# A written-out order for the second attention front and the inverse steps ahead of it

## The chip, the core and the metric

The kernel runs on one core of a Trainium2 chip. Its time is the device time of one execution in microseconds (us). The kernel before was run 12 times: the median is 447.94 us, the lowest 445.24, the highest 451.13. One execution was also recorded by the profiler.

The engines that matter here are TensorE (PE in the views; PEld is its weight load), VectorE (DVE), ScalarE (ACT), GpSimd (POOL) and SyncE (SP, which issues the DMAs). Each works through its own instructions in the order in which the program lists them, and waits at an instruction until what it needs is there.

## What is computed

Four layers work on `x`, 2048 rows of 512 columns, in turn: attention, convolution, attention, convolution, each on the layer-normed `x` and added to it.

```python
x = x + _A_ref(_layernorm(x), A_wqkv, A_wo)          # attention: 32 heads of 16, window of 8 keys, dilation 2
x = x + _B_ref(_layernorm(x), ...)                   # long convolution per column, by FFT
x = x + _A_ref(_layernorm(x), A_wqkv, A_wo)
x = x + _B_ref(_layernorm(x), ...)
```

The kernel does the convolution as matrix products with Fourier factors: two forward steps, a pointwise product, two inverse steps. The change is about the seam between the first convolution's inverse steps and the second attention's first part.

## The kernel before

**The convolution's end.** `FftB` keeps the 512 columns as two groups `g` of 256. The first inverse step (`i1`, L781, written "y" in the order strings) makes one of 8 tiles per group: 16 matmuls (L792, L793) into one PSUM tile of 128 x 1024 f32, then one eviction (`evac`, L708, traced as L709) into `z`. I number these tiles y0 to y15; y0 to y7 belong to group 0 and y8 to y15 to group 1. (Group 0's `z` lies in the buffer `xnT`, so the profile calls it `xnT`.)

The second inverse step (`i2`, L797, "z") makes one of 4 blocks of 512 rows for one group; I write z10 for group 1, block 0. It needs all eight y tiles of its group. It comes in two forms. With "D", 8 matmuls (L808, L809) are followed by an addition on VectorE that adds the PSUM tile to `x_sb` (L812). With "A", 4 matmuls by the identity (L807) put `x_sb` into the sum first, and ScalarE copies the 12-matmul result back (L814).

**PSUM.** All y and z tiles come from two pools, "right" and "left", of two such tiles each, used two by two in turn (`ptile`, L704). A tile can be started when the tile that had its buffer is evicted. `swap_psum` (L848) gives the right pool up, and the front's tiles (two for transposes, two for projections) take its place.

**The attention's front.** For each block `b` of 512 rows: the statistics of each half of the columns (`half_stats`, L99: 4 instructions, L101), the mean and variance (`aggr`, L1283), the reciprocal root by Ln and Exp on ScalarE (`rstd_act`, L104), the normalisation on VectorE (`norm`, L1291, traced as L136 and 4 of L148), 16 transposes on TensorE in two tiles (`front_t`, L209; L215) with one eviction each (L218), four key projections of 4 matmuls each (`front_k`, L224; L229) with an eviction on ScalarE each (L232), and a shifted copy of the keys for the window (`front_ext`, L234; L242). The queries of a block are four projections of the same size (`qproj1`, L168; L172) with an eviction on ScalarE each (L174). The logits are then made in `core` (L295): `mult` (L277; L283, 2.3 us on VectorE) and `lsum` (L286; L290, 32 small matmuls) for each block and quarter of the columns.

I use the same short names for both kernels: h10 are the statistics of group 1 in block 0, a0, p0 and n0 the aggregation, root and normalisation of block 0, T0 its transposes, E00 and E01 their two evictions, P00 to P03 its key projections, Q00 to Q03 its query projections, x0 and e0 its shifted copies (e for the last block, by quarter), mult 00 and L00 the first product and the first logit sum.

**What sets the order.** VectorE, ScalarE, TensorE and SyncE are listed in `MAN`: they take their instructions exactly as the Python code calls them. The convolution's calls come from a string of tokens (`ORDER0`) that `run` (L819) walks through. Its last line ends in

```python
yA m m yA m yA yD yD yD yD yD zD yA yA zD yA yA zD zD zD
```

where A and D say whose eviction it is. Behind it the front is written as Python: `i2(1, 1)`, statistics, normalisation and so on block after block, with one of each block's transpose evictions on ScalarE and one on VectorE, and 4 spare matmuls (`warm`, L193; L195) after the first transposes. Block 3's keys and block 0's queries are called from `core`'s events around the first `mult`s.

Of the kernel before, what the change touches and what calls it, by code (L numbers as in the profile page):

```python
# [14 lines left out]
F32 = mybir.dt.float32  # L15
# [5 lines left out]
P = 128  # L21
S = 2048
D = 512
# [4 lines left out]
NDT = 4  # L28
# [9 lines left out]
NG = 2  # L38
DQG = 64
EC = 16  # L40
NEC = 128 // EC
# [3 lines left out]
KA KD KA KD KA KA KD KA KD KA KD kA KD KA KA kD kA kD kA UA KD UA UA UD UA kD UA  # L45
UA UD KA UA kD u kD m u u u kA m UA m UD UA u kA m kD u UA u m UA m
UD m UA kA u kD kD u kA u m m kA m u u yD yA m u u m u m yA u yA
yA m m yA m yA yD yD yD yD yD zD yA yA zD yA yA zD zD zD
"""
ORDER1 = """  # L50
UD UA UA UD UA UA UD UA UD UA UD u UD u m UA u u m UA m u u UA m UD m
u u m m m u u m u m m u u m u m m u yA yA yA m u yA yA yA yA
m yD yA yD yD yA zD yD yA zD yA yA zD zD zD zD zA zB
"""

def build_a_consts(tc, nc, cpool, tpool):
# [42 lines left out]
def half_stats(nc, lnst, x_sb, t, g):  # L99
    for a in range(4 * t, 4 * t + 4):  # L100
        nc.vector.bn_stats(lnst["bn"][:, a, g, :], x_sb[:, a, g * (D // 2):(g + 1) * (D // 2)])  # L101
# [49 lines left out]
class LayerA:  # L151
# [31 lines left out]
    def front_open(self):  # L183
        tc = self.tc
        self.fctx = ExitStack()
        l = self.layer
        self.fp = self.fctx.enter_context(tc.tile_pool(name=f"a{l}_front", bufs=2, side="right"))
        self.ps_tr = self.fctx.enter_context(tc.tile_pool(name=f"a{l}_ps_tr", bufs=2, space=PSUM, side="right"))
        self.ps_pj = self.fctx.enter_context(tc.tile_pool(name=f"a{l}_ps_pj", bufs=2, space=PSUM, side="right"))
        self.pj_tag = "pp"  # L190
        self.nc.gpsimd.memset(self.kT[:, :, 0:14, 0:1], 0.0)

    def warm(self, ps, n, rhs):  # L193
        for _ in range(n):
# [11 lines left out]
        for a in range(4):  # L206
            ln_apply(self.nc, self.xn[:, a, :], x_rows[:, a, :], rn[0], rn[1], a, ln_eng[a])

    def front_t(self, b, ev_eng, defer=False):  # L209
        nc, xn, evs = self.nc, self.xns.pop(b), []  # L210
        for dp in range(2):
            pt = self.ps_tr.tile([P, 2, 4, P], BF16, name="pt")
            for di in range(2):
                for a in range(4):
                    nc.tensor.transpose(pt[:, di, a, :], xn[:, a, (2 * dp + di) * P:(2 * dp + di + 1) * P], self.c["ident"][:])  # L215
            dst = self.xnT[:, 2 * dp:2 * dp + 2, b * 512:(b + 1) * 512]
            f = nc.scalar.copy if ev_eng[dp] == "act" else nc.vector.tensor_copy
            evs.append(lambda f=f, dst=dst, pt=pt: f(dst, pt[:].rearrange("p t a q -> p t (a q)")))  # L218
        if not defer:
            for f in evs:  # L220
                f()
        return evs

    def front_k(self, b, ev_eng, fts=range(NDT)):  # L224
# [445 lines left out]
class FftB:  # L670


    def __init__(self, tc, nc, C, ident, w2_dram, g2_dram, kf_dram, x_sb, tag):
        self.tc, self.nc, self.C, self.ident, self.kf_dram, self.x_sb = tc, nc, C, ident, kf_dram, x_sb
        self.w2_dram, self.g2_dram = w2_dram, g2_dram
        self.tag = tag
        self.c_grp, self.c_mid, self.c_ps = ExitStack(), ExitStack(), ExitStack()
        self.grp = self.c_grp.enter_context(tc.tile_pool(name=f"b{tag}_grp", bufs=5, reuse_waits="tile"))
        self.ps = [c.enter_context(tc.tile_pool(name=f"b{tag}_ps_{side}", bufs=2, space=PSUM, side=side))
                   for c, side in ((self.c_ps, "right"), (self.c_grp, "left"))]  # L680
        self.npt = 0
        self.kf, self.nat, self.ub = {}, {}, {}
        self.nkf = 0
        g2p = self.c_grp.enter_context(tc.tile_pool(name=f"b{tag}_g2", bufs=1, reuse_waits="tile"))
        self.g2 = g2p.tile([P, 2, 16, P], BF16, name="g2_sb")
        self.S = [dict() for _ in range(NG)]
# [107 lines left out]
        self.evac(z[:, :, t * DQT * 4:(t + 1) * DQT * 4].rearrange("p m (j d) -> p m j d", d=4),  # L794
                  p3[:].rearrange("p j (m d) -> p m j d", d=4), eng)

    def i2(self, g, t, eng="dve", defer=False):  # L797

        nc, x_sb = self.nc, self.x_sb
        z = self.S[g]["z"]  # L800
        dsl = slice(g * DQG * 4, (g + 1) * DQG * 4)
        p4 = self.ptile([P, 4, DQG * 4])
        n_add = {"dve": 4, "both": 2, "act": 0}[eng]
        for j in range(4):
            a = t * 4 + j
            if j >= n_add:
                nc.tensor.matmul(p4[:, j, :], lhsT=self.ident[:], rhs=x_sb[:, a, dsl], start=True, stop=False)  # L807
            nc.tensor.matmul(p4[:, j, :], lhsT=self.g2[:, 0, a, :], rhs=z[:, a, :], start=(j < n_add), stop=False)  # L808
            nc.tensor.matmul(p4[:, j, :], lhsT=self.g2[:, 1, a, :], rhs=z[:, NA + a, :], start=False, stop=True)  # L809
        if n_add:  # L810
            xr = x_sb[:, t * 4:t * 4 + n_add, dsl]
            nc.vector.tensor_tensor(xr, p4[:, 0:n_add], xr, ALU.add)  # L812
        if n_add < 4:
            ev = lambda: nc.scalar.copy(x_sb[:, t * 4 + n_add:t * 4 + 4, dsl], p4[:, n_add:4])  # L814
            if defer:
                return ev
            ev()

    def run(self, order, u, done=lambda g, t: None, k=None, late=()):  # L819
        late, cnt = list(late), {}  # L820
        src = dict(K=("ka", k), U=("ua", u))
        self.nk, self.nm = (0, 0) if k is not None else (NG * NEC, 0)
        self.pump()
        for tok in order.split():
            op, eng = tok[0], dict(A="act", D="dve", B="both").get(tok[1:])
            n = cnt[op] = cnt.get(op, -1) + 1
            g, t = divmod(n, 4 if op == "z" else 8)
            if op in src:
                key, x = src[op]
                self.f1(g, x, key, t, eng)  # L830
                if op == "K":
                    if n > 0 and late:
                        late.pop(0)()
                    if n == NG * NQT - 1:
                        self.open_ring()
            elif op == "k":
                self.k_f2(g, t, eng)
            elif op == "u":
                self.u_f2(g, t)
            elif op == "m":  # L840
                self.u_mult(g, t)
            elif op == "y":
                self.i1(g, t, eng)
            else:
                self.i2(g, t, eng)
                done(g, t)

    def swap_psum(self):  # L848
        self.c_ps.close()
# [14 lines left out]
def k_gen(tc, nc, ident, ins, kd, la, x_v, lnst, b_consts, C):  # L864
# [4 lines left out]
    with ExitStack() as ctx:  # L869
# [3 lines left out]
        c0 = pw.tile([P, 2, 4 * P], BF16, name="c_t")  # L873
        xb, ln = {}, {}
        la.front_open()

        def x_load(b):
            xb[b] = la.fp.tile([P, 4, D], BF16, name="x_blk")
# [13 lines left out]
            la.front_apply(b, xb[b], ln[b], [eng] * 4, xb[b])  # L892

        def front(b):
            la.front_t(b, ["act"] * 2)
            if b == 0:
                x_load(2)
            la.front_k(b, ["act"] * 4)
            if b < 3:
                la.front_ext(b, "dma")  # L900
# [267 lines left out]
def kernel(  # L1168
# [92 lines left out]
    fb.ahead = 4  # L1261
    fb.open_mid()
    with tc.manual_schedule(engines=MAN):
        def half(g, t):
            if g == 0 and t < 2:
                half_stats(nc, lnst, x_sb, t, 0)

        fb.run(ORDER0, u, half, kp, late)
    fb.c_mid.close()
    la.close()  # L1270
    la = LayerA(tc, nc, consts, lnst, A_wqkv, A_wo, 1, xnT, 1)
    la.front_w()
    with tc.manual_schedule(engines=MAN):
        fb.swap_psum()
        la.front_open()
        ln, agg = {}, {}

        def stats(b):
            half_stats(nc, lnst, x_sb, b, 1)
            if b > 1:  # L1280
                half_stats(nc, lnst, x_sb, b, 0)

        def aggr(b):  # L1283
            agg[b] = lnp.tile([P, 4, 2], F32, name="ln_ag")
# [6 lines left out]
        def norm(b):  # L1291
            la.front_apply(b, x_sb[:, b * 4:(b + 1) * 4, :], ln_end(nc, lnp, ln[b]), ["dve"] * 4)

        def keys(b, *fts):
            la.front_k(b, ["act"] * 4, fts)

        fb.i2(1, 1, "act")
        stats(0)
        aggr(0)
        power(0)  # L1300
        fb.i2(1, 2, "act")
        ev3 = fb.i2(1, 3, "act", True)
        norm(0)
        pt = la.front_t(0, ("act", "dve"), True)
        stats(1)
        pt[0]()
        pt[1]()
        ev3()
        la.warm(la.ps_pj.tile([P, 512], F32, name="pp", tag=la.pj_tag), 4, la.wqk[:, 0, 0:512])
        for b in range(3):  # L1310
            if b == 0:
                aggr(1)
                power(1)
                norm(1)
            keys(b, 0, 1, 2)
            pt = la.front_t(b + 1, ("act", "dve"), True)
            pt[0]()
            if b < 2:
                stats(b + 2)
            pt[1]()  # L1320
            keys(b, 3)
            if b < 2:
                aggr(b + 2)
                power(b + 2)
                norm(b + 2)
            if b > 0:
                la.front_ext(b - 1, "dve")
        la.front_ext(2, "dve")
        la.front_close()
        fb.c_ps.close()  # L1330
        fb.c_grp.close()
        krctx.close()

        def last(*fts):
            for ft in fts:
                keys(3, ft)
                la.qproj1(0, ft, la.qT[0], la.ps_pj, la.pj_tag)

        ext = lambda ft: lambda: la.front_ext(3, "dve", ft)
        ev = {("m", 0, ft): [ext(ft)] for ft in range(NDT)}  # L1340
        ev[("m", 0, 0)].insert(0, lambda: last(0, 1))
        ev[("q", 0, 0)] = [lambda: last(2)]
        ev[("q", 0, 1)] = [lambda: last(3)]
        ev[("p", 8)] = [lambda: la.load_w2(w2_dram)]
        la.core(x_sb, u, lnp, ev)
    la.close_logits()

# [49 lines left out]
```

## Time and profile before

| | us |
|---|---|
| median of 12 runs | 447.94 |
| profiled execution, its own time | 447.13 |
| its span, first to last instruction | 445.3 |
| TensorE busy in the span | 349.2 |
| VectorE busy | 407.4 |
| ScalarE busy | 320.5 |
| GpSimd busy | 45.1 |
| granted TensorE clock, mean | 0.987 |

The seam lies at about 256 to 303 us of the span. The y tiles of group 0 end near 260 us, those of group 1 near 270 us; the first `mult` of the second attention starts at 297.83 us. The median time of one instruction, from the groups of that stretch:

| operation | engine | ns |
|---|---|---|
| y eviction, 128 x 1024 f32 from PSUM | VectorE | 1215 |
| the same | ScalarE | 1015 |
| z addition (D form) | VectorE | 1211 |
| z copy (A form) | ScalarE | 1008 |
| transpose eviction | VectorE / ScalarE | 680 / 1014 |
| key or query eviction, 128 x 512 f32 | ScalarE | 583 |
| one half-statistic (4 for an h) | VectorE | 413 |
| one normalisation (4 for an n) | VectorE | 410 |

An instruction's recorded time is longer than its distance from the next, since the engines overlap the end of one with the start of the next: four y evictions in a row on ScalarE took 3.80 us, so the next follows after some 0.93. How to read the views: a row of the timeline is the start, the time taken, the engine and line, what is written from what, a count, and in brackets the idle time before it with what ended it.

### The profile page before, as it was taken

How to read it: one execution, taken by the hardware profiler on the slowest of the kernel's cores; microseconds unless marked ns; L12 is line 12 of the kernel's file. 1: busy time of each engine (PE TensorE's matmuls, PEld its weight loads, DVE VectorE, ACT ScalarE, POOL GpSimd, SP SyncE). 2: the span in 40 equal slices, each digit the busy share in tenths (PEclk: the TensorE clock that was granted, in tenths of full speed). 3: DMA queues.
4: the chain of work that ended last, by engine and by line, in shares of the span. 5: the costliest groups of instructions: out<-in, count | busy, mean ns of one | idle time of the engine just before them, and what ended most of it. 6: DMA issues, size and time to landing. Idle time of an engine off the chain costs nothing.

```text
span 445.3 us, 12704 instructions
## 1 busy us (share of the span) xinstructions
PE 349.2 (78%) x5455; PEld 265.3 (60%) x5494; DVE 407.4 (91%) x563; ACT 320.5 (72%) x538; POOL 45.1 (10%) x46
## 2 busy tenths in 40 slices
PE   1000045879999998999897898999999899998795
PEld 1000024566676577787787796545657687867694
DVE  6799999999999999998789999879999999889974
ACT  5979989686555559888999963764655459679862
POOL 2000101100089400000400000000000020000000
PEclk9999997999999999999999999999999899999999
DMA  7930641121411575480266730850033056224405
GB/s 207 373 114 14 69 70 27 46 55 21 103 17 41 150 252 163 129 353 16 112 231 226 254 121 24 244 159 3 2 83 85 0 202 236 87 97 133 155 25 166
DMA packets 65354, 54.17 MB, mean 122 GB/s; under 512 B 36781, under 2 KB 53778, under 8 KB 64018
## 3 DMA queue, kind: packets, MB, share of 16 engines
q1 hardware_dynamic: 65154, 53.22, 39.0%
q8 instruction: 43, 0.70, 0.7%
q10 hardware_dynamic: 144, 0.13, 0.1%
q14 instruction: 13, 0.11, 0.1%
HBM read 30.28 MB, written 13.24 MB: 98 GB/s over the span
## 4 chain that ended last, share of the span: by engine, by line
PE 32%; DVE 19%; ACT 11%; DMA 5%; issue 3%; SPq 2%; DVEq 0%; ACTq 0%
PE po L395 9%; DVE prod L283 5%; PE pq L407 4%; ACT a1s L709 4%; PE pq L336 3%; PE pq L172 3%; PE L L290 2%; DVE pav L387 2%; DVE ln_bn L101 2%; DVE t L767 2%; DMA kf_ring<-kf_dram 2%; PE pb L792 2%; PE pb L793 2%; ACT ub L779 2%; PE pp L229 2%
## 5 line engine op out<-in xcount | busy, mean ns | idle before, releaser
L387 DVE TENSOR_TENSOR pav<-attn,v_ext 128x4096 bf16<-128x4096 bf16 x32 | 72.8, 2284 | 0.5 <-DMA v_ext<-v_ext 0.2
L283 DVE TENSOR_TENSOR prod<-qT,kT_ext 128x4096 bf16<-128x4096 bf16 x29 | 66.5, 2309 | 1.1 <-ACT qT L174 0.6
L395 PEld LDWEIGHTS <-pav 128*128 128x128 bf16 x1024 | 60.4, 99 | 10.9 <-DVE pav L387 6.5
L395 PE MATMUL po<-ident,pav 128*128 128x128 bf16 x1024 | 64.0, 222 | 3.6 <-DVE pav L387 3.6
L215 PE MATMUL pt<-ident,x_blk 128*128 128x128 bf16 x64 | 5.6, 241 | 45.2 <-ACT x_blk L146 45.2
L229 PE MATMUL pp<-xnT,kT_ext 128*128 128x512 bf16 x124 | 30.5, 384 | 5.9 <-ACT xnT L218 3.8
L779 ACT CAST ub<-pb 128x1024 bf16<-128x1024 f32 x32 | 33.0, 1089 | 2.2 <-DVE t L767 2.1
L129 POOL TENSOR_TENSOR ln_rstd<-ln_rstd,ln_mh 128x4 f32<-128x4 f32 x6 | 10.0, 1658 | 233.1 <-DVE ln_rstd L128 211.1
L792 PE MATMUL pb<-Wp,t 128*128 128x128 bf16 x256 | 30.2, 219 | 2.7 <-ACT ub L779 2.2
L215 PEld LDWEIGHTS <-x_blk 128*128 128x128 bf16 x64 | 4.4, 108 | 46.3 <-ACT x_blk L146 46.0
L290 PEld LDWEIGHTS <-prod 128*128 128x128 bf16 x928 | 27.1, 96 | 8.1 <-DVE prod L283 2.5
L338 ACT CAST v_ext<-pq 128x512 bf16<-128x512 f32 x32 | 18.7, 586 | 18.0 <-PE pq L336 17.7
L727 PE MATMUL pb<-a1s,w_sb 128*128 128x64 bf16 x768 | 27.1, 193 | 5.7 <-ACT ub L779 3.5
L1092 PE MATMUL pk<-B_t,A_t 128*64 128x84 bf16 (+1 forms) x512 | 25.5, 211 | 6.6 <-issue 4.4
L336 PE MATMUL pq<-wv,xnT 128*128 128x512 bf16 x119 | 30.3, 379 | 0.4
L398 ACT CAST oT<-po 128x512 bf16<-128x512 f32 x32 | 18.6, 580 | 16.4 <-PE po L395 16.2
L172 PE MATMUL pq<-xnT,kT_ext 128*128 128x512 bf16 x121 | 30.0, 379 | 0.4 <-issue 0.2
L709 ACT CAST a1s<-pb 128x1024 bf16<-128x1024 f32 x30 | 29.3, 1079 | 1.3 <-PE pb L720 1.3
L793 PE MATMUL pb<-WpJ,t 128*128 128x128 bf16 x256 | 30.2, 219 | 0.0
L407 PE MATMUL pq<-wop,oT 128*128 128x512 bf16 x110 | 29.3, 379 | 0.9
L727 PEld LDWEIGHTS <-w_sb 128*128 128x128 bf16 x768 | 24.7, 98 | 8.1 <-issue 7.0
L1092 PEld LDWEIGHTS <-A_t 128*64 128x64 bf16 (+1 forms) x512 | 23.3, 111 | 9.7 <-issue 6.2
(222 smaller groups left out, 878.0 us busy)
## 6 DMA issues: line engine op xcount, KB each, us to landing
w_sb<-w_dram SPq DMA_DIRECT2D x8, 1024.0 KB
w_dram<-w_zero SPq DMA_DIRECT2D x1, 4096.0 KB
kf_ring<-kf_dram SPq DMA_DIRECT2D x13, 256.0 KB
kf_ring<-kf_dram SPq DMA_DIRECT2D x26, 128.0 KB
v_ext<-v_ext SPq DMA_DIRECT2D x4, 784.0 KB
x_blk<-in_A_x_dram SPq DMA_DIRECT2D x4, 512.0 KB
kT_ext<-in_A_wqkv_dram SPq DMA_DIRECT2D x4, 512.0 KB
x_sb<-in_A_x_dram SPq DMA_DIRECT2D x4, 512.0 KB
```

The lines of the kernel that those rows point to most:

```text
L172: nc.tensor.matmul(pq[:], lhsT=self.wqk[:, dt, ft * P:(ft + 1) * P], rhs=self.xnT[:, dt, q * 512:(q + 1) * 512], start=(dt == 0), stop=(dt ...
L229: nc.tensor.matmul(pp[:], lhsT=self.wqk[:, dt, D + ft * P: D + (ft + 1) * P], rhs=self.xnT[:, dt, b * 512:(b + 1) * 512], start=(dt == 0), ...
L283: nc.vector.tensor_tensor(pr, self.qT[q][:, ft].unsqueeze(1).to_broadcast([P, W, 4, P]), kap, ALU.mult)
L336: nc.tensor.matmul(pp[:], lhsT=xnT[:, dt, a * P:(a + 1) * P], rhs=wv[:, dt, :], start=(dt == 0), stop=(dt == NDT - 1))
L387: nc.vector.tensor_tensor(pv[:], attn[:, n % 4].unsqueeze(2).to_broadcast([P, W, DH, H]), vap, ALU.mult)
L395: nc.tensor.matmul(po[:, ft, :], lhsT=pvf[:, w, ft * P:(ft + 1) * P], rhs=ident[:], start=(w == 0 and ft == 0), stop=(w == W - 1), skip_gr ...
L407: nc.tensor.matmul(pw[:], lhsT=oT[:, ftp, :], rhs=wo[:, ftp, :], start=False, stop=(ftp == NDT - 1))
L709: (self.nc.scalar.copy if eng == "act" else self.nc.vector.tensor_copy)(dst, src)
L727: nc.tensor.matmul(p2[:, j, :], lhsT=self.w2[:, ec * EC + j, :], rhs=a1s[:, ec * EC + j, :], start=True, stop=True)
L779: nc.scalar.copy(ub[:], p2)
L792: nc.tensor.matmul(p3[:, j, :], lhsT=t1[:, dql, :], rhs=wp_r, start=True, stop=False)
L1092: nc.tensor.matmul(o, lhsT=lhs, rhs=Bt[:, ri, c * CH + ql].rearrange("p b g -> p (b g)"), start=(not half and j % 4 == 0 and ri == 0), sto ...
```

## The change

The end of `ORDER0` is cut off after y7, and everything up to the first `mult` is one string, `ORDERF`, that the same `run` walks through; `more` maps the front's tokens to its calls. In the tokens a digit pair after z is group and block, after h too; after E it is block and half, after P block and quarter.

```diff
-yA m m yA m yA yD yD yD yD yD zD yA yA zD yA yA zD zD zD
+yA m m yA m yA yD
+"""
+ORDERF = """
+yA yA yA yA yA yA z00D yA h00 yA z01D h01 z10A z11A h10 a0 p0 h11
+n0 z12A z02A a1 z03A h12 S T0 h02 p1 E00A n1 E01A a2 z13A P00 h13 Q00
+h03 T1 E10A p2 E11D P01 a3 P02 P03 P10 p3 P11 n2 n3 P12 T2 E20D E21A
+P13 T3 E30A P20 P21 x1 P22 P23 E31D
...
-        fb.run(ORDER0, u, half, kp, late)
+        fb.run(ORDER0, u, k=kp, late=late)
...
-        fb.i2(1, 1, "act")
-        stats(0)
-        aggr(0)
-        power(0)
-        fb.i2(1, 2, "act")
-        ev3 = fb.i2(1, 3, "act", True)
-        norm(0)
-        pt = la.front_t(0, ("act", "dve"), True)
...
-        la.warm(la.ps_pj.tile([P, 512], F32, name="pp", tag=la.pj_tag), 4, la.wqk[:, 0, 0:512])
...
+        front = dict(S=front_pools, h=lambda g, t: half_stats(nc, lnst, x_sb, t, g), a=aggr, p=power, n=norm, T=transposes,
+                     E=lambda b, d, eng: pts[b][d](eng), P=lambda b, ft: la.front_k(b, ["act"] * 4, (ft,)),
+                     Q=lambda q, ft: la.qproj1(q, ft, la.qT[q], la.ps_pj, la.pj_tag), x=lambda b: la.front_ext(b, "dve"),
+                     e=lambda ft: la.front_ext(3, "dve", ft))
+        fb.run(ORDERF, None, more=front)
...
-        ev = {("m", 0, ft): [ext(ft)] for ft in range(NDT)}
-        ev[("m", 0, 0)].insert(0, lambda: last(0, 1))
-        ev[("q", 0, 0)] = [lambda: last(2)]
-        ev[("q", 0, 1)] = [lambda: last(3)]
-        ev[("p", 8)] = [lambda: la.load_w2(w2_dram)]
+        ev = {("p", 8): [lambda: la.load_w2(w2_dram)]}
+        ev["m", 0, 0] = [last(("P", 3, 0), ("P", 3, 1), ("x", 0), ("x", 2), ("P", 3, 2), ("Q", 0, 1), ("e", 0), ("Q", 0, 2))]
+        ev["m", 0, 1] = [last(("e", 1), ("e", 2))]
+        ev["m", 0, 2] = [last(("e", 3))]
+        ev["q", 0, 0] = [last(("P", 3, 3), ("Q", 0, 3))]
```

So the four y tiles y8 to y11 and the three blocks z02, z03 and z10 go from VectorE to ScalarE; z10 and z11 come ahead of z02 and z03; block 0's second transpose eviction goes from VectorE to ScalarE, and block 2's two evictions change places (E20 on VectorE, E21 on ScalarE); block 0's first query projection is made in the front; and the 4 spare matmuls are gone. `front_open` is split so that the front's PSUM pools open at S, after z03. The order of the DMAs on SyncE's queue and of the work on GpSimd is the same in both kernels. `ORDER1`, the last convolution's string, is rewritten with explicit block numbers, in the same order as before.

## The prediction

> **What bounds the kernel now.** I read the busy table by stages first. Its columns are the length of the stretch, then busy time and count of each engine, then the granted clock.
>
> ```profile
> core 0: us, PE busy (x) PEld busy (x) DVE busy (x) ACT busy (x) POOL busy (x), PEclk, DMA share, GB/s
> 266.00:272.00 6.00, 5.44 (x66) 4.89 (x64) 5.93 (x12) 2.95 (x4) 0.00 (x0) 1.00 0.00 0
> 277.00:298.00 21.00, 18.67 (x127) 10.01 (x130) 17.62 (x59) 14.07 (x26) 0.00 (x0) 1.00 0.76 227
> 298.00:334.00 36.00, 35.58 (x489) 21.23 (x496) 33.85 (x26) 19.96 (x36) 0.00 (x0) 1.00 0.10 27
> ```
>
> At 266 to 272 VectorE is full and ScalarE half idle. At 277 to 298 none is full: the blocks hand over from one to another. Behind 298 TensorE is full. So the seam's worth is the time at which TensorE has its work behind it. The timelines tell who is late. VectorE:
>
> ```profile
> 260.90 4.61 DVE L709 CAST z<-pb 128x1024 bf16<-128x1024 f32 x4
> 270.56 3.47 DVE L812 TENSOR_TENSOR x_sb<-pb,x_sb 128x1024 bf16<-128x1024 f32 x3
> 274.06 1.41 DVE L101 BATCH_NORM_STATS2 ln_bn<-x_sb 128x6 f32<-128x256 bf16 x4
> 297.83 2.29 DVE L283 TENSOR_TENSOR prod<-qT,kT_ext 128x4096 bf16<-128x4096 bf16 x1 [0.62 <-ACT qT L174]
> ```
>
> It evicts y8 to y11, then, after z00 and z01, adds z02, z03 and z10 in one run; h10, the start of the front's chain, waits for all that until 274.06. ScalarE meanwhile:
>
> ```profile
> 257.50 3.80 ACT L709 CAST xnT<-pb 128x1024 bf16<-128x1024 f32 x4
> 265.10 1.93 ACT L709 CAST z<-pb 128x1024 bf16<-128x1024 f32 x2 [3.80 <-PE pb L793]
> 273.32 1.01 ACT L814 CAST x_sb<-pb 128x1024 bf16<-128x1024 f32 x1 [3.62 <-PE pb L809]
> ```
>
> Two holes of 3.80 and 3.62 us. The first row also gives its pitch: 0.93 us for each eviction. TensorE:
>
> ```profile
> 271.81 0.27 PE L807 MATMUL pb<-x_sb,ident 128*128 128x256 bf16 x1 [0.56 <-DVE x_sb L812]
> 276.97 1.87 PE L215 MATMUL pt<-ident,xn 128*128 128x128 bf16 x16 [1.06 <-DVE xn L148]
> 278.67 1.03 PE L195 MATMUL pp<-kT_ext,ident 128*128 128x512 bf16 x3
> 285.57 2.32 PE L229 MATMUL pp<-xnT,kT_ext 128*128 128x512 bf16 x10 [0.92 <-DVE xnT L218]
> 291.20 2.32 PE L229 MATMUL pp<-xnT,kT_ext 128*128 128x512 bf16 x10 [1.01 <-DVE xnT L218]
> 299.54 1.03 PE L172 MATMUL pq<-xnT,kT_ext 128*128 128x512 bf16 x4
> 302.93 0.22 PE L290 MATMUL L<-ind,prod 128*128 128x8 bf16 x3
> ```
>
> It waits for a PSUM buffer, for n0, and in two blocks for a transpose eviction that VectorE makes behind 8 statistics. From y15's last matmul to L01 (268.47 to 302.93) it takes 34.46 us. Its work there, by pitches of the same timeline (z of 8 matmuls 0.88, of 12 1.31, T 0.95, a projection 0.864, L00 0.80): 3 x 0.88 + 3 x 1.31 + warm 0.86 + 4 x 0.95 + 20 x 0.864 + 0.80 = 29.3. So **5.1 us are idle**.
>
> **The change, part by part.** I place the new order by those pitches, an instruction starting when its engine and its inputs are ready (a TensorE tile's result is there some 0.16 behind its pitch).
>
> *y8 to y15 on ScalarE.* It is free of y6 at 261.2 and takes y8 to y13 at 0.93 to 266.8. TensorE makes a y in 0.917 and is held to that by PSUM anyway: y8 starts at 259.5, y13 at 264.1, z00 at 265.0, y14 at 265.9, y15 at 266.8, z01 at 267.7 to 268.6. y14 and y15 are evicted at 267.0 and 267.9 to 268.95 (in the trace 269.7). Here a rule speaks against the change: the Trainium skill ("TensorEngine Tiling (Array Packing)", PSUM Bottleneck) wants both engines for evicting PSUM. Two evictors at pitches of 1.13 (the row of 4.61 for four) and 0.93 would take a tile each 0.51, 8 tiles in 4.1 us; one takes 7.4. By the rule the change loses 3.3 us. But TensorE delivers only one tile in 0.917, so one evictor at 0.93 keeps up; by the rows it costs about 0.1 and I take that.
>
> *z10 first.* TensorE z10 waits for y15 (0.4 us idle), 269.0 to 270.3; ScalarE copies it 270.5 to 271.5. VectorE, done with h01 at 271.3, starts **h10 at 271.5 instead of 274.06**. Price: z02, z03 and z10 get 4 identity matmuls each, 12 x 0.109 = 1.3 us of TensorE.
>
> *What eats most of that.* ScalarE goes z11 (271.75), p0 (273.3), z12, z02, z03 (to 276.7). VectorE: a0 to 273.2, h11, then n0 274.75 to 276.05. TensorE: z11, z12, z02, z03 to 275.5, T0 from 275.6. So T0 gains 1 us, not 2.6. The pools' swap adds a wait at T0 for z12 and z02 (evicted by 275.6), which z03 covers; without that cover T0 would be 0.1 later.
>
> *Both first evictions on ScalarE.* Queued behind z03 and p1: E00 277.0, E01 277.9 to 278.9; z13 fills TensorE meanwhile. P00 starts 278.1 and gets its second half at 279.0 (0.5 idle). In the trace P00 starts at 279.54, dense after the spare matmuls. So P00 is some 1 us ahead.
>
> *Dense from there.* Q00 to 280.3; n1 (VectorE: a1, h12, h02, n1) ends 280.7, so T1 idles 0.35; P01 to P03 to 284.0; P10's second half needs E11, which VectorE makes after h13 and h03, at 284.25, just when asked for; P11, P12 to 286.6; n2 ends 286.15, so T2 is not held; P13; n3 287.65; T3 needs E20 off VectorE (288.3), starts 288.4; P20 to P23 to 292.8; P30 to 293.65. ScalarE's evictions fit between (2 projection buffers; none late by over 0.1). P30's copy ends 294.4, e0 follows, **mult 00 at 294.8 instead of 297.83**.
>
> *The spare matmuls.* Gone: -0.86. The nearest rule is the Trainium skill's clock gate ("TensorE: Matmul & The Clock Gate", The HAM clock gate): TensorE falls to half rate after an idle window of some 3.4 us and stays there about as long. By it a cold start at T0 would stretch 3.4 us of matmuls by some 1.7 us (an estimate from that page). The rows: clock 1.00 throughout, longest idle 1.06; the new order's longest is about 0.5. I take nothing; the far end is +1.7.
>
> *Behind mult 00.* P31, P32, Q01, Q02, P33, Q03 follow on TensorE to 298.85, L00 to 299.65. mult 00 ends 297.0, e1, e2, mult 01 297.7, e3, mult 02 300.3, mult 03 302.5 (trace 305.69). From then on both kernels do the same, with TensorE full.
>
> *Moved past.* SyncE's and GpSimd's orders are unchanged. The value weights' load waits for z13 (275.6, now 277.9); its first reader is at 308.0, new 305, and all DMAs of that burst took 20 us, this one being first: covered. ORDER1 is the same order: nothing.
>
> The sum, on TensorE: work -0.86 + 1.3; start 268.6 (z01 now behind y15) for 268.47; idle 0.4 + 0.1 + 0.2 + 0.5 + 0.35 = about 1.5 for 5.1. That is +0.44 + 0.13 - 3.6 = **-3.0**; mult 00 says the same. The rest of the kernel follows its own triggers, so it shifts whole. Profiled execution: 447.13 - 3.0 = 444.1. Its time is 0.8 under the median of 447.94, so against that I put **444.9**.
>
> **Rivals.**
>
> *Handovers eat it.* The new chain is tight at n2 (0.45 spare), n3/E20 (0.1), P10 and P12. If each of the four block starts loses 0.5 us, as instructions with two waits might, 2.0 of 3.0 go: 446.9. For it: nothing full in 277 to 298 today. Against: durations there repeat within 0.02 us, and today's idle of 0.92 and 1.01 has a named cause, 8 statistics before the eviction, which the new order takes apart.
>
> *ScalarE becomes the pace.* It alone releases y8 to z13 and E00/E01: 16 evictions in one queue ahead of P00. Where ScalarE follows a projection it sits idle 0.28 before each today; if these ran at 1.01 + 0.28 = 1.29 instead of 0.93, E01 and so P00 come 16 x 0.36 = 5.8 later, for a net of +2.8: **450.7, slower**. It decides from a pitch of 0.93 + 3.0/16 = 1.12. Against: the run of four at 3.80, and TensorE tiles already waiting when ScalarE gets to them.
>
> *It is given back later.* TensorE's 35.58 of 36 moves along, but a transfer that doesn't would hold it: the copy of the values ends at 340.9 and VectorE waits for it 0.17. It is started by the values' last eviction, so it moves too. If it didn't: 447.9.
>
> **How the numbers follow.** Dense front (444.9): 0.62, own range 443.4 to 446.4. Handovers (446.9): 0.20. ScalarE's pace (450.7): 0.11. Given back (447.9): 0.07. What can be told from no change here is 0.5%, 2.24 us: faster is below 445.7, slower above 450.2. Faster: 0.53 of the first case and 0.05 of the second, 0.58. Slower: 0.09 of the third, and 0.01 each of the second, with a clock loss of 1.7, and of the fourth: 0.11. The rest, 0.31, is no change. The range, 443.2 to 448.4, leaves out the ScalarE case and the tails.
>
> **What would show it.** Right: eight L709 rows on ScalarE at 0.93 without a hole; h10 at about 271.5; T0 near 275.6; TensorE busy over 95% from 279 to 299; first L283 near 294.8; later L283 and L395 shifted by the same 3 us. Wrong: gaps before T2 or T3 named L148 or L218; ScalarE rows at 1.1 or more; a granted clock under 1.00; a first L283 at 294.8 with an end that hasn't moved.

## The result, and the profile after

The new kernel's median is 444.77 us (12 runs, 440.87 to 448.21). The old kernel, timed again beside it, has a median of 448.33 us over 49 runs. The ratio of their times is 0.9903, with a 95% interval of 0.9876 to 0.9929: **3.2 to 5.6 us shorter**. The ratio leaves out one run of each kernel (448.21 and 452.38 us) that lies more than 1.5% above that kernel's fastest. 444.9 was forecast, from a gain of 3.0.

The profiled execution of the new kernel hides this. It took 446.95 us, with a span of 445.2 against the old 445.3. A late transfer (the kernel's last swapped filter block, `kf_nat`) held VectorE for 1.45 us just ahead of y7's eviction, and TensorE for 1.36 us in y8, so the seam began late. To compare I measure the **seam**: from the start of VectorE's eviction of y7, the last instruction that both kernels share, to the start of mult 00. In the old profile it is 297.83 - 259.76 = 38.07 us:

```profile
259.76 1.23 DVE L709 CAST xnT<-pb 128x1024 bf16<-128x1024 f32 x1 [0.27 <-PE pb L793]
```

VectorE's timeline of the new kernel:

```profile
262.34 1.22 DVE L715 CAST xnT<-pb 128x1024 bf16<-128x1024 f32 x1
268.87 1.23 DVE L818 TENSOR_TENSOR x_sb<-pb,x_sb 128x1024 bf16<-128x1024 f32 x1 [5.31 <-PE pb L815]
272.79 2.80 DVE L107 BATCH_NORM_STATS2 ln_bn<-x_sb 128x6 f32<-128x256 bf16 x8
281.67 1.38 DVE L154 TENSOR_SCALAR xn<-x_sb,ln_rstd,ln_nb 128x512 bf16<-128x512 bf16 x4
285.88 0.68 DVE L226 COPY xnT<-pt 128x1024 bf16<-128x1024 bf16 x1
297.21 2.29 DVE L289 TENSOR_TENSOR prod<-qT,kT_ext 128x4096 bf16<-128x4096 bf16 x1
```

The seam is 297.21 - 262.34 = **34.87 us, 3.2 less**. The four z casts are gone from VectorE (it idles 5.31 us there), and h10 runs right behind h01, in the row of 8. ScalarE of the same kernel:

```profile
263.53 5.59 ACT L715 CAST z<-pb 128x1024 bf16<-128x1024 f32 x6 [0.84 <-PE pb L799]
269.76 1.93 ACT L715 CAST z<-pb 128x1024 bf16<-128x1024 f32 x2 [0.64 <-PE pb L799]
276.30 1.91 ACT L820 CAST x_sb<-pb 128x1024 bf16<-128x1024 f32 x2
279.64 1.91 ACT L226 COPY xnT<-pt 128x1024 bf16<-128x1024 bf16 x2
```

The six follow each other at 0.90 us (the last of them takes 1.07, so 5.59 = 5 x 0.90 + 1.07). That is less than the 0.93 worked out above, which took too little for a row's last eviction, and less than TensorE's 0.917 for a tile: one engine keeps up. TensorE's timeline:

```profile
278.25 1.36 PE L224 MATMUL pt<-ident,xn 128*128 128x128 bf16 x16
281.60 0.59 PE L235 MATMUL pp<-xnT,kT_ext 128*128 128x512 bf16 x2 [0.45 <-ACT xnT L226]
282.89 1.12 PE L224 MATMUL pt<-ident,xn 128*128 128x128 bf16 x16
283.85 5.34 PE L235 MATMUL pp<-xnT,kT_ext 128*128 128x512 bf16 x24
291.68 6.21 PE L235 MATMUL pp<-xnT,kT_ext 128*128 128x512 bf16 x28
```

The waits for n0 (1.06 in the old rows), for VectorE's transpose evictions (0.92 and 1.01) and for a PSUM buffer (0.56) are gone. One of 0.45 remains, for E01; z10 waits 0.3 for y15, and n0 still spaces T0 out: z13 follows 1.20 us behind T0's start, where a dense T takes 0.89. 24 and 28 projection matmuls run without a gap. The busy table by stages (length, busy time and count of each engine, granted clock, DMA):

```profile
core 0: us, PE busy (x) PEld busy (x) DVE busy (x) ACT busy (x) POOL busy (x), PEclk, DMA share, GB/s
267.00:272.00 5.00, 4.86 (x70) 4.48 (x67) 3.10 (x6) 4.05 (x5) 0.00 (x0) 1.00 0.01 3
279.00:299.00 20.00, 19.44 (x139) 11.16 (x139) 15.80 (x47) 16.19 (x30) 0.00 (x0) 1.00 0.76 221
299.00:334.00 35.00, 34.58 (x495) 21.00 (x501) 32.73 (x26) 18.84 (x34) 0.00 (x0) 1.00 0.13 38
```

TensorE is busy 97% of 279 to 299, where it was 89% of the old 277 to 298.

### The profile page after: what moved, and what is told of

It is laid out like the page before. It is cut to its first block, busy times and chain, and to the rows that moved or that the text cites. A ratio compares the mean times of both kernels' runs of the same rounds, so it can differ in the third digit from the quotient of the medians.

```text
span 445.2 us, 12719 instructions
## 1 busy us (share of the span) xinstructions
PE 350.1 (79%) x5463; PEld 266.3 (60%) x5502; DVE 398.7 (90%) x555; ACT 327.6 (74%) x546; POOL 45.0 (10%) x46
## 4 chain that ended last, share of the span: by engine, by line
PE 52%; ACT 14%; DVE 11%; DMA 6%; issue 2%; SPq 1%; DVEq 0%; ACTq 0%
PE po L401 9%; PE pq L342 6%; PE pp L235 5%; PE pq L178 5%; PE pk L1103 5%; PE L L296 5%; PE pq L413 4%; ACT a1s L715 4%; DVE pav L393 3%; DMA v_ext<-v_ext 3%; PE pb L798 2%; PE pb L799 2%; ACT ub L785 2%; ACT xnT L226 2%; DMA kf_ring<-kf_dram 1%
## 5 line engine op out<-in xcount | busy, mean ns | idle before, releaser
L180 ACT CAST qT<-pq 128x512 bf16<-128x512 f32 x32 | 18.6, 583 | 15.1 <-PE pq L178 14.7
```

## The experiments

All seams and the stretch from mult 00 to the end of the span, in us, each from one profiled execution. The ratio is to the old kernel, where timed, with its interval. The seam repeats well: the four profiles of old fronts (old, e6, e8, e10) lie within 0.02 us, e4 and e11 agree at 34.57.

| kernel | seam | behind mult 00 | ratio |
|---|---|---|---|
| old | 38.07 | 147.5 | |
| new | 34.87 | 148.0 | 0.9903 (0.9876 to 0.9929) |
| e1: old, evictions moved | 37.63 | 147.3 | 0.9963 (0.9929 to 0.9996) |
| e2: new order, old engines | 37.99 | 148.3 | 0.9990 (0.9964 to 1.0016) |
| e3: new, z02 and z03 ahead of z10 | 38.13 | 147.2 | 0.9983 (0.9959 to 1.0007) |
| e4: new again | 34.57 | 145.9 | 0.9916 (0.9885 to 0.9946) |
| e5: new, 4 spare matmuls | 35.43 | 145.9 | 0.9926 (0.9904 to 0.9947) |
| e6: old, 4 spare matmuls more | 38.06 | 148.4 | |
| e7: new, one more h03 | 35.57 | 146.1 | |
| e8: old, no spare matmuls | 38.08 | 147.8 | |
| e9: e3, 8 spare matmuls | 36.78 | 145.8 | |
| e10: old, spare matmuls in the attention | 38.07 | 146.8 | |
| e11: new, the same | 34.57 | 145.9 | 0.9884 (0.9843 to 0.9926) |

### Which part of the change does it: e1 and e2

e1 is the old kernel with the new kernel's engines for y8 to y11, z02, z03 and z10.

```diff
-yA m m yA m yA yD yD yD yD yD zD yA yA zD yA yA zD zD zD
+yA m m yA m yA yD yA yA yA yA zD yA yA zD yA yA zA zA zA
```

> The old kernel with the evictions of y8 to y11, z02, z03 and z10 on ScalarE, everything behind as it was. The seam is measured from the start of VectorE's eviction of y7 to the start of mult 00: 38.07 us in the old kernel, 34.87 in the new one. Theory (engines and order are needed together): with z02 and z03 still ahead of z10, h10 comes only 0.35 us earlier and the front behind it keeps its gaps, so the seam is 37.7 and the time is unchanged within 0.2%. Rival (relief of VectorE alone is the gain): seam 35.5 or less, time 0.6% shorter.

The seam is 37.63: 0.44 of the 3.2. VectorE's timeline of e1 shows what became of its freed time:

```profile
269.91 1.41 DVE L101 BATCH_NORM_STATS2 ln_bn<-x_sb 128x6 f32<-128x256 bf16 x4
275.41 1.41 DVE L101 BATCH_NORM_STATS2 ln_bn<-x_sb 128x6 f32<-128x256 bf16 x4 [4.10 <-ACT x_sb L814]
```

It stands still for 4.10 us ahead of h10, because z10 is third in TensorE's and ScalarE's queues. The whole kernel is 0.37% shorter (0.04 to 0.71), a little more than the 0.2% expected; that interval doesn't exclude the rival's 0.6%, but the seam does, which the rival put at 35.5 or less.

e2 keeps the new order and gives the evictions back to VectorE.

```diff
-yA yA yA yA yA yA z00D yA h00 yA z01D h01 z10A z11A h10 a0 p0 h11
-n0 z12A z02A a1 z03A h12 S T0 h02 p1 E00A n1 E01A a2 z13A P00 h13 Q00
+yD yD yD yD yA yA z00D yA h00 yA z01D h01 z10D z11A h10 a0 p0 h11
+n0 z12A z02D a1 z03D h12 S T0 h02 p1 E00A n1 E01A a2 z13A P00 h13 Q00
```

> The new order with the old engines: y8 to y11, z10, z02 and z03 evicted by VectorE again. Theory (both are needed together): VectorE has 8.1 us of evictions back, 2.3 of them ahead of n1, so T1 waits and the seam is about 38.0 us, no gain over the old 38.07. Rival (the order alone is the gain, VectorE has room): seam 35.5 or less.

The seam is 37.99, as worked out. E01, E20, E21, Q00 and the statistics stay as in the new kernel. TensorE's and VectorE's timelines of e2:

```profile
279.07 1.89 PE L224 MATMUL pt<-ident,xn 128*128 128x128 bf16 x16 [3.88 <-DVE x_sb L818]
```

```profile
276.50 1.38 DVE L154 TENSOR_SCALAR xn<-x_sb,ln_rstd,ln_nb 128x512 bf16<-128x512 bf16 x4
277.80 1.22 DVE L818 TENSOR_TENSOR x_sb<-pb,x_sb 128x1024 bf16<-128x1024 f32 x1
279.26 1.17 DVE L818 TENSOR_TENSOR x_sb<-pb,x_sb 128x1024 bf16<-128x1024 f32 x1
280.35 2.70 DVE L107 BATCH_NORM_STATS2 ln_bn<-x_sb 128x6 f32<-128x256 bf16 x8
283.15 1.38 DVE L154 TENSOR_SCALAR xn<-x_sb,ln_rstd,ln_nb 128x512 bf16<-128x512 bf16 x4
```

T0 waits 3.88 us until VectorE has added z02, whose PSUM buffer it takes over, and n1 comes behind both additions and 8 statistics. It is n1 that sets the seam, as expected: P01 starts 0.79 us behind the end of n1 (0.80 in e4). The granted clock (1.00 is full rate) fell to 0.50 behind T0's wait, from 278.60 to 282.01 us, which I had not expected; it cost the seam nothing here, because n1 ended later still. So **neither half is worth much by itself**: 0.44 and 0.08 us alone, 3.2 to 3.5 together.

e2 also shows where the loss is not. z00's addition, first in e2 and then in e4 (the new kernel again, see below):

```profile
266.92 1.22 DVE L818 TENSOR_TENSOR x_sb<-pb,x_sb 128x1024 bf16<-128x1024 f32 x1 [0.49 <-PE pb L815]
266.75 1.23 DVE L818 TENSOR_TENSOR x_sb<-pb,x_sb 128x1024 bf16<-128x1024 f32 x1 [5.01 <-PE pb L815]
```

That is 6.23 us into the seam in both, and z01's addition starts at 8.89 in both. Whether VectorE evicts y8 to y11 or ScalarE evicts all eight makes no difference up to there. What costs are z02 and z03, which VectorE adds between n0 and n1.

### Whether the first rows have to come first: e3 and e9

e3 puts z02 and z03 ahead of z10 and z11 in the new kernel, with their statistics.

```diff
-yA yA yA yA yA yA z00D yA h00 yA z01D h01 z10A z11A h10 a0 p0 h11
-n0 z12A z02A a1 z03A h12 S T0 h02 p1 E00A n1 E01A a2 z13A P00 h13 Q00
-h03 T1 E10A p2 E11D P01 a3 P02 P03 P10 p3 P11 n2 n3 P12 T2 E20D E21A
+yA yA yA yA yA yA z00D yA h00 yA z01D h01 z02A z03A h02 z10A h03 z11A h10 a0 p0 h11
+n0 z12A a1 h12 S T0 p1 E00A n1 E01A a2 z13A P00 h13 Q00
+T1 E10A p2 E11D P01 a3 P02 P03 P10 p3 P11 n2 n3 P12 T2 E20D E21A
```

> The new kernel with z02 and z03 ahead of z10 and z11 again, their statistics h02 and h03 moved forward with them, all on ScalarE. Theory: h10 starts 2.3 us later, TensorE waits that much longer at T0, and part comes back because h02 and h03 are out of the later chain: seam 36.9 us, 2.0 more than the new 34.87. Rival (which rows come first does not matter, since TensorE's sum of work is the same): seam 34.9 to 35.2.

The seam is 38.13: the order of the z blocks matters, and by 1.2 us more than I had worked out. TensorE waits for n0, as expected:

```profile
280.31 2.53 PE L224 MATMUL pt<-ident,xn 128*128 128x128 bf16 x16 [2.23 <-DVE xn L154]
282.64 0.42 PE L813 MATMUL pb<-x_sb,ident 128*128 128x256 bf16 x1
282.86 0.42 PE L814 MATMUL pb<-z,g_sb 128*128 128x256 bf16 x1
```

But the transposes then take 2.53 us, where the old kernel's, fed row by row by n0 as well, took 1.87, and z13's first matmuls follow at 0.22 instead of 0.11. The table by stages of the same kernel gives the granted clock (behind the five engines):

```profile
280.00:282.00 2.00, 1.53 (x10) 1.02 (x11) 2.00 (x10) 0.38 (x2) 0.00 (x0) 0.60 0.01 4
282.00:284.00 2.00, 2.00 (x16) 1.64 (x15) 1.96 (x8) 1.96 (x3) 0.00 (x0) 0.55 0.03 8
```

e9 tests this on e3: 8 spare matmuls (a new token w, its definition left out) in that wait.

```diff
-n0 z12A a1 h12 S T0 p1 E00A n1 E01A a2 z13A P00 h13 Q00
+n0 z12A a1 h12 S w T0 p1 E00A n1 E01A a2 z13A P00 h13 Q00
```

> The kernel of e3 (z02 and z03 ahead of z10) with 8 spare matmuls of 128 x 512, 1.73 us, in TensorE's 2.23 us wait ahead of T0; their result is not read. Theory (e3 lost 1.2 us more than worked out because the granted clock fell to 0.55 to 0.60 in T0 and z13 behind that wait): the clock stays 1.00 and the seam falls from 38.13 to 36.9 us. Rival (e3's extra 1.2 us are a wait that the work missed): 38.1.

```profile
280.00:282.00 2.00, 2.00 (x11) 0.91 (x10) 1.84 (x10) 2.00 (x3) 0.00 (x0) 1.00 0.20 23
```

The clock stays at 1.00 and the seam is 36.78, against 36.9 worked out for e3. So the z order, with h02 and h03, costs 36.78 - 34.57 = 2.2 us by itself. Of the 1.35 us between e3 and e9, 0.29 is a late transfer as in the first new profile (e3's z00 starts 6.53 us into the seam, e9's 6.24), and the other 1.06 is the clock's. The mean clock of e3's 20 timed runs is 0.986, against 0.990 in 54 runs of the old kernel beside them; one half-rate stretch takes 1.7 of some 446 us, 0.004, so the fall in the seam is no accident of one profile (e2's 12 runs have 0.985).

e9 has the rest of the change and is 1.3 us under the old seam. How that splits over the evictions, E01, E20 and E21, Q00 and the order of the statistics no run shows.

### Who is full in the new front, and what was idle in the old one: e5 to e8

e5 puts 4 spare matmuls (token w, whose definition is left out here) between P13 and T3 of the new kernel, e6 the same behind block 1's last key projection in the old one.

```diff
-P13 T3 E30A P20 P21 x1 P22 P23 E31D
+P13 w T3 E30A P20 P21 x1 P22 P23 E31D
```

> The new kernel with 4 spare matmuls of 128 x 512 (0.86 us of TensorE) added between P13 and T3; their result is not read. Theory (TensorE is the full engine of the new front): the seam grows by the whole 0.86, from 34.87 to 35.7 us. Rival (VectorE or ScalarE sets the pace): it grows by 0.3 or less.

```diff
             keys(b, 3)
+            if b == 1:
+                la.warm(la.ps_pj.tile([P, 512], F32, name="pp", tag=la.pj_tag), 4, la.wqk[:, 0, 0:512])
```

> The old kernel with the same 4 spare matmuls behind block 1's last key projection; their result is not read. Theory: they lie in the 1.01 us in which TensorE waits for block 2's transpose eviction, so the seam stays 38.07 us within 0.2. Rival (TensorE was the limit before as well): seam 38.9.

e5: 35.43, 0.86 above e4, the whole of it. e6: 38.06, nothing. Its TensorE (L195 are the spare matmuls):

```profile
291.33 1.03 PE L195 MATMUL pp<-kT_ext,ident 128*128 128x512 bf16 x4
292.20 3.06 PE L229 MATMUL pp<-xnT,kT_ext 128*128 128x512 bf16 x12
```

They fill most of the 1.01 us that the old kernel waits there for an eviction. The new front has no such place.

e7 makes h03 twice, so that VectorE has 1.33 us more ahead of n2.

```diff
-h03 T1 E10A p2 E11D P01 a3 P02 P03 P10 p3 P11 n2 n3 P12 T2 E20D E21A
+h03 T1 E10A p2 E11D P01 a3 P02 P03 P10 p3 P11 h03 n2 n3 P12 T2 E20D E21A
```

> The new kernel with the statistics h03 made a second time ahead of n2, 1.33 us more for VectorE. Theory (VectorE has 0.1 to 0.7 us to spare at n2, n3 and E20, so it is nearly as full as TensorE): seam 36.1 us, 1.2 more. Rival (VectorE has room now that the evictions are gone): within 0.3 of 34.87.

35.57, 1.0 above e4: of the 1.33 us VectorE had 0.3 to spare there. T3 shows the wait in TensorE's timeline:

```profile
289.35 1.05 PE L224 MATMUL pt<-ident,xn 128*128 128x128 bf16 x16 [0.32 <-DVE xnT L226]
```

So the new front is tight on two engines at once, TensorE and VectorE. e8 takes the 4 spare matmuls out of the old front:

```diff
-        la.warm(la.ps_pj.tile([P, 512], F32, name="pp", tag=la.pj_tag), 4, la.wqk[:, 0, 0:512])
```

> The old kernel without its 4 spare matmuls in the front. Theory: block 0's keys then wait for E01 instead, to 279.8 in the old timeline, and the later waits stay, so the seam is 38.0 us and the granted clock 1.00 through it. Rival (they keep the clock up): rows of the front at half rate, some 1.7 us more.

38.08, with a clock of 1.00 from 270 to 290 us. They neither cost nor brought anything in the old kernel.

### The spread, and what lies behind the seam: e4, e10 and e11

e4 is the new kernel again.

> The new kernel unchanged, for the spread of its profile on the same chip. Theory: the seam is 34.9 us again within 0.2, and what lies before and behind it varies by 2 us or so from one execution to the next. Rival (the gain sits elsewhere, since the first profiled spans are 445.3 and 445.2): the seam moves by a us or more, or the stretch behind mult 00 is shorter than the old 147.5.

```profile
260.52 1.22 DVE L715 CAST xnT<-pb 128x1024 bf16<-128x1024 f32 x1 [0.27 <-PE pb L799]
295.09 2.29 DVE L289 TENSOR_TENSOR prod<-qT,kT_ext 128x4096 bf16<-128x4096 bf16 x1
```

The seam is 34.57. The 0.3 against the first profile is that profile's late transfer: there TensorE stood in y8 until 0.14 us into the seam, so that z00 was added 6.53 us into it, against 6.23 here. Behind mult 00 e4 takes 145.9 us, against 147.5 in the old profile and 148.0 in the new one. I had called that stretch the same. Of the 1.6 us to the old profile, 1.25 lie in the second attention, from the third product with the values to the last: 41.79 us in e4, 43.04 in the old profile, 43.11 in the new one. TensorE at the fourth product, first in the old kernel, then in e4:

```profile
348.67 3.49 PE L395 MATMUL po<-ident,pav 128*128 128x128 bf16 x32 [1.25 <-DVE pav L387]
345.74 1.96 PE L401 MATMUL po<-ident,pav 128*128 128x128 bf16 x32 [1.24 <-DVE pav L393]
```

In both it waits some 1.25 us. Behind the wait the old kernel's clock falls to half, and e4's doesn't. The table by stages, again the old kernel first:

```profile
345.09:348.50 3.41, 2.13 (x39) 1.25 (x37) 3.41 (x2) 2.18 (x6) 0.00 (x0) 1.00 0.00 0
348.50:351.92 3.42, 3.25 (x31) 3.26 (x32) 3.42 (x4) 0.00 (x0) 0.00 (x0) 0.50 0.00 0
351.92:355.33 3.41, 3.36 (x37) 2.34 (x36) 3.41 (x2) 2.47 (x6) 0.00 (x0) 1.00 0.00 0
```

```profile
342.06:345.48 3.42, 2.23 (x41) 1.34 (x39) 3.42 (x2) 2.28 (x6) 0.00 (x0) 1.00 0.00 0
345.48:348.89 3.41, 3.10 (x38) 2.44 (x40) 3.41 (x4) 0.66 (x2) 0.00 (x0) 1.00 0.00 0
```

The half rate lasts 3.41 us. Five of e4's 19 timed runs took 447.79 us or more, and none lies between 445.7 and 447.7; no profile caught one of them, so what they lose is open. e10 and e11 put 5 spare matmuls into the wait for the fourth product, in the old and the new kernel (the line is e11's).

```diff
+        ev["o", 2] = [lambda: la.warm(la.ps_pj.tile([P, 512], F32, name="pq", tag=la.pj_tag), 5, la.wqk[:, 0, 0:512])]
```

> The old kernel with 5 spare matmuls (1.08 us) in the second attention, in the 1.25 us in which TensorE waits for the fourth product with the values; their result is not read. Six profiles of kernels with a seam of 37.6 us or more all have a half-rate stretch behind that wait and 147.2 to 148.4 us behind mult 00; three of four with the new seam have none and 145.9 to 146.1. Theory (the wait is what lets the clock fall): granted clock 1.00 from 340 to 360 us and 146.1 us behind mult 00, the seam 38.07. Rival (the clock falls by chance or for another cause): a clock of 0.83 to 0.9 in ten us of it again, 147.3 or more.

> The new kernel with the same 5 spare matmuls in the second attention; their result is not read. Theory: seam 34.6 to 34.9 us, no half-rate stretch, 146.0 us behind mult 00, and a time at or up to 1 us under the new kernel's (ratio to the old kernel 0.988 to 0.992). Rival (the spare matmuls delay what follows them): 147 us or more behind mult 00 and a ratio of 0.993 or more.

Of e10:

```profile
349.00:351.00 2.00, 1.95 (x37) 1.09 (x36) 2.00 (x2) 1.19 (x4) 0.00 (x0) 1.00 0.00 0
```

The clock is 1.00 and the stretch of the products 41.79 us. Behind mult 00 it is 146.8 us, between the two expectations, since from the first to the third product with the values it took 8.60 us, against 7.98 in the old profile. That piece varies by up to 1.1 us between the thirteen profiles (7.73 to 8.86); in most of the long ones VectorE waits there for the copy of the values. e11 has the seam of 34.57 and 145.85 us behind. Its median of 442.66 (6 runs, 442.39 to 443.84) is the lowest of all. Its interval of 0.9843 to 0.9926 lies clear of the old kernel but overlaps that of the new one, so that e11 beats the new kernel isn't shown.

The clock fell at the fourth product in seven profiles without these spare matmuls (old, new, e1, e2, e3, e6, e8) and not in four (e4, e5, e7, e9). All six with the old seam's length have it, and one of four with the new, which looks as if the shorter seam changed the odds. The traces say otherwise. The granted clock changes on a grid of 3.41 us: in e2 and in e3 the fall in the seam and the fall here start 71.68 us apart (278.60 and 350.28, 280.40 and 352.08), 21 times 3.413, and the rows above, cut at the grid, are at 1.00 or 0.50 throughout. Where the grid lies differs from execution to execution. In the seven, the wait began 1.04 to 2.33 us behind a grid point, so that it lay in one interval (all but 0.17 us at most) together with the 32 small matmuls ahead of it, and the clock fell at the interval's end. In the four it began 0.68, 0.70, 2.43 and 3.35 us behind one, and wait or small matmuls were shared between two intervals. That fits all eleven, though no run shifted the grid on purpose. The wait is the same in both kernels, so nothing ties the fall to the shorter seam; by these bounds it comes in 38 to 51% of executions, if the grid lies anywhere with equal chance (an estimate from 1.29 to 1.73 of 3.41 us). The mean clock of the timed runs agrees: 0.990 in the old kernel, 0.990 in the new one's 12 runs, 0.988 in e4's 19.

e10's spare matmuls start 2.09 us behind a grid point, where the clock fell in the other profiles, so that profile counts for them. e11's start 0.73 us behind one, and it might have kept the clock without them.

## Why the prediction was right

*What bounds the seam.* Right. The sum was made on TensorE's idle time, and e5 and e6 show that it is the quantity: 0.86 us of extra work counts in full in the new front and nothing in the old.

*y8 to y15 on ScalarE.* Right: 7.70 us for eight in e4, and z00 comes at 6.23 us with one engine evicting or with two (e4, e2). The rule that both engines should evict would have made the change a loss of 3.3 us at this place; TensorE's 0.917 us for a tile is what decides. The 0.1 us that the prediction charged isn't there, since the true pitch is 0.90.

*h10, T0, P00, T1, T2, T3, mult 00.* Against the start of y7's eviction the forecast put T0 at 15.8, P00 at 18.3, T1 at 20.5, T2 at 26.8, T3 at 28.6 and mult 00 at 35.0 us. e4 has 15.6, 18.1, 20.3, 26.4, 28.1 and 34.6. The terms that made it 0.2 to 0.5 too long are z10, which ends 10.3 us into e4's seam where 10.5 was forecast (0.2), the wait at T1 (0.35 forecast, about 0.1 measured) and the transposes' pitch (0.95, where dense ones took 0.89). The signs were given as times of the span (T0 near 275.6, mult 00 near 294.8), and the first profile misses them by its late start: T0 at 278.25, mult 00 at 297.21. e4 has 276.14 and 295.09.

*z10 first.* Right that it is needed: e9 prices it at 2.2. How much is eaten before T0 was put too high. The prediction says that T0 gains 1 us, but its own times (275.6 for 276.97) give 1.4, and e4 has 1.6 (15.6 us into the seam for the old 17.2).

*The spare matmuls.* Right for this change, where the longest wait left is 0.45 us. All five profiles of the new order (new, e4, e5, e7, e11) kept the clock at 1.00 through it. But the prediction counted the clock's fall as a far end that needs an idle window of 3.4 us, and e3 shows it behind a wait of 2.23 us, with TensorE busy for 1.18 of the 3.41 us ahead of the fall. The margin was smaller than the prediction said.

*The rivals.* Handovers: n2 and E20 are as tight as stated (e7), and they held. ScalarE's pace: excluded by the pitch. Given back later: not as a rule. The third product with the values, which needs the copy, starts 42.91 us behind mult 00 in e4 and 43.10 in the old profile; in the first new profile the copy held VectorE for 0.72 us (0.17 in the old one) and it was 43.51, so 0.4 us went back in that execution.

*The size.* 3.0 was forecast, the seam gave 3.2 and 3.5, and the whole kernel 3.2 to 5.6, so the seam alone can account for it. The half-rate stretch in the second attention is worth 1.3 us where it falls, but the mean clocks of the timed runs don't show it less often in the new kernel, so it is no part of the gain that I can show. That the median of 444.77 lies 0.1 from the forecast is luck: the same kernel's 19 runs in e4 have 443.80. The prediction's statement that both kernels do the same behind mult 00 holds for the instructions; the clock differs from execution to execution.

## What to carry to other kernels

Before a change of order at a seam, place each instruction by the pitches in the timeline and sum the waits of the engine that is full behind the seam: that gave the gain within 0.5 us. Moving work to an idle engine and moving the first consumer's input forward may each be worth little alone (0.44 and 0.08 us here), so test them together before rejecting one. Compare the stretch that was changed, from a shared instruction to a shared instruction, since the spans of two profiles can hide 3 us.

## What the runs showed of the hardware

The granted clock of TensorE fell to half behind waits much shorter than the idle window that the Trainium skill ("TensorE: Matmul & The Clock Gate", The HAM clock gate) names, of some 3.4 us: behind 2.23 us in e3 and, in seven of eleven profiles, behind 1.25 us in the second attention. In these places the half rate lasted 3.41 us each time, as that page has it. It began and ended on a grid of 3.41 us that lies differently in each execution, and the 1.25 us wait lost the clock when it lay in one interval of the grid together with the small matmuls ahead of it. There TensorE was busy for 1.97 to 2.14 us of the interval, so not idle throughout.

Matmuls whose result nobody reads, put into the wait, went with a clock of 1.00 in all three profiles where they were tried. In e9 and e10 they stood where the clock fell without them, and in e9 that was worth 1.06 us of seam.

ScalarE evicted tiles of 128 x 1024 f32 from PSUM at a distance of 0.90 us, VectorE at 1.13, though one alone takes 1.01 and 1.22. With TensorE making a tile in 0.917, ScalarE alone kept up.
